# Two V loads and one V shift moved in the DMA order of a streaming-attention and feed-forward kernel

## The chip, the cores and the metric

One core of a Trainium2 chip runs the whole program. The metric is the device time of one execution in microseconds (us), as the median over executions. The engines are PE (TensorE), DVE (VectorE), ACT (ScalarE), POOL (GpSimd) and SP (SyncE). POOL and SP matter here because they issue DMAs: each takes its instructions strictly in order, so a DMA that waits for a semaphore holds up all that stands behind it.

## The reference

Attention over 4 batches, 8 heads, 768 positions and a head size of 64, then a feed-forward layer over the 3072 rows:

```python
scores = q @ k^T / 8                                # per batch and head
mask   = causal                       # heads 0, 2, 6 ("retrieval")
mask   = causal & (first 4 keys | last 64 keys)     # the other five ("streaming")
a      = softmax(where(mask, scores, -1e9))
x      = (a @ v), heads side by side                # [3072, 512]
h      = x @ w_in                                   # [3072, 2048]
out    = max(0.01 * h, h) @ w_out                   # [3072, 512]
```

## The kernel before

The rows are cut into eight chunks of 384 positions, two for each batch; chunk 4 is the first half of batch 2, chunk 5 its second half. A chunk passes through these stages: K, Q and V are loaded (converted to bf16), three pieces of 128 positions each; K and Q are turned, that is transposed, by DMA; K is spread by DVE into the score operand; the scores, their exponent and mask, and the product with V run on PE, ACT and DVE; the attention output is turned by DMA into `xt`; the two feed-forward products follow on PE.

The feed-forward products of earlier chunks are woven between the attention of the next one. That order is written out by hand: in pass n of the main loop the string `WOVEN[n]` (lines 602 to 609) names, letter by letter, the next piece of work from a list. In pass 3, `a` is an attention step of chunk 4, `t`, `A` and `B` are input products of chunk 3, `p` is an output product of chunk 2, `e` is the spreading of one third of chunk 5's K (line 274, DVE), and `v` is `v_shift(5)`.

V stands in two layouts. `va` is what `load_v` (line 118) loads on POOL's queue. `vb` is the same V moved by 64 positions, made by `v_shift` (line 146) with two DMAs, lines 150 and 151, for the streaming heads, whose window starts 64 positions early. `v_shift(4)` is issued on POOL, `v_shift(5)` on SP.

Two single buffers set the order of the loads: there is one `kb` and one `qb`, so the load of the next chunk's K waits until the present K has been turned, and the same for Q. `load_v` can take `behind=`: then POOL first copies one element of the tile named (line 121, into `hold`), and so waits until that tile has been written. Loads (`load_qk`, `load_v`) are on POOL's queue; turns (`turn_dma`, line 245), the turned attention outputs (line 443), the output stores (line 868) and most shifts are on SP's.

Around the change POOL's order is: load K and Q of chunk 4, load V of chunk 4 (line 1151), the sink values of batch 2 (line 133), `v_shift(4)`, load K and Q of chunk 5 (these in pass 2), then in pass 3 load V of chunk 5, load K of chunk 6, wait for the last output `xt` of chunk 4 (line 1187), load Q and V of chunk 6. SP's order in pass 3 is: turn K and Q of chunk 5, the four turned outputs of chunk 4 (heads 0 and 1, 2 and 3, 4 and 5, 6 and 7; here outputs 0 to 3), with stores between them, and `v_shift(5)` behind the fourth.

Behind output 3, pass 4 forms `x_sums` of chunk 4 on DVE (line 662), which read all four outputs; the product with `vb` of chunk 5 comes soon after (line 336).

Of the kernel before, what the change touches and what calls it, by code (L numbers as in the profile page):

```python
# [21 lines left out]
def kernel(  # L22
# [73 lines left out]
    raw = {}  # L96
# [13 lines left out]
    def load_qk(n, nms="kq"):  # L110
        b, c = ORDER[n]
        for nm in nms:
            t = rot.tile([128, 3, H, D], BF16, name=f"{nm}b", tag=f"{nm}b", bufs=1)
            raw[nm, n] = t
            for g in range(3):
                nc.gpsimd.dma_start(out=t[:, g], in_=nat[nm][b, c, :, :, g])  # L116

    def load_v(n, gs=range(3), behind=None):
        b, c = ORDER[n]
        if behind is not None:  # L120
            nc.gpsimd.tensor_copy(hold[0:1, :], behind)
        for g in gs:
            nc.gpsimd.dma_start(out=va[b][:, 3 * c + g, :, 0:D], in_=nat["v"][b, c, :, :, g])  # L123
# [3 lines left out]
    def load_sinks(b, eng=None):  # L127
        vsf[b] = vsfs[b % 2]
        (eng or nc.sync).dma_start(out=vsf[b].rearrange("(r f) d -> r f d", f=4)[:, 0], in_=v[b, :, 0:NS, :])

    def sink_values(b, eng):
        n = H - 1
        eng.tensor_tensor(
            vs[b % 2][:, 1:H, 0:D],
            vsf[b].rearrange("p (o d) -> p o d", o=1).to_broadcast([128, n, D]),
            m_sink[:, 1:H].rearrange("p (h o) -> p h o", o=1).to_broadcast([128, n, D]),
            op=ALU.mult)
# [8 lines left out]
    def v_shift(n, eng=None):  # L146
        eng = eng or nc.sync
        i, c = ORDER[n]
        lo, hi = (0, 2) if c == 0 else (2, 5)
        eng.dma_start(out=vb[i][0:64, lo:hi], in_=va[i][64:128, lo:hi, 1:H])  # L150
        eng.dma_start(out=vb[i][64:128, lo:hi], in_=va[i][0:64, lo + 1 : hi + 1, 1:H])
# [93 lines left out]
    def turn_dma(n, nms="kq"):  # L245
        for nm in nms:
            dst = rot.tile([128, 3, 4, 128], BF16, name=f"{nm}d", tag=f"{nm}d", bufs=3 if nm == "q" else 2)
            if nm == "q":
                qx[n] = dst
            else:  # L250
                raw["kx", n] = dst
            thirds = [slice(j, j + 1) for j in range(1 if nm == "q" and n == 3 else 3)]
            for g in thirds if n < 4 or (nm, n) == ("k", 4) else [slice(0, 3)]:
                nc.sync.dma_start_transpose(out=dst[:, g].rearrange("p g q t -> p (g q) t"),
                                            in_=raw[nm, n][:, g].rearrange("p g h d -> p (g h d)"))
# [8 lines left out]
    def spreads(n):  # L264
        b, c = ORDER[n]

        def spread(g, hh):
            r = slice(64 * hh, 64 * hh + 64)
            o = CH * c + 128 * g
            dst, src = kt[b % 2][hh][r, :, o : o + 128], raw["kx", n][r, g]  # L270
            if n == 2 and hh:
                nc.scalar.activation(out=dst, in_=src, func=ACTF.Copy)
            else:
                nc.vector.tensor_copy(dst, src)

        order = [(g, hh) for hh in range(2) for g in range(3)] if n < 4 else [(g, hh) for g in range(3) for hh in range(2)]
        r = [lambda g=g, hh=hh: spread(g, hh) for g, hh in order]
        if c == 0:
            r += sink_keys_by(b)
        return r  # L280
# [210 lines left out]
    class First:  # L491
# [109 lines left out]
    FIRST = "tttttttDttttL0tttt10Wt0kkk4k10k00k1k1S000k00S00aav011aSa22aa1Sa1a11a1aT1a11aa22a2a2eeaea2ee2eaa"  # L601
    WOVEN = {
        2: "aaptpIataatataatataqIataItaattIaaetaeapeaatatateaaepetteppe",
        3: "aappapapaxAppptAAaaAAtpAatAaaptaaBBAptpeeBaapaBBvetpBBpetetBe",
        4: "paappapapaxppaaApaatapatAaapAapAaAtpAaAeaeBpteeapapetaaABpeptpaBpBepatBptBpevBppppBpp",
        5: "paaxAteaAeatpaaAAtpIAaappaABApaatpBppeatBaeAIppaIeBBptpBItBtpBev",
        6: "axapAaApApaAAppApAaBapBBaAaBBpaaBpBapaCCaaCpaCBCapapCaaCDpapapDapppDpaDDpppDDDCppppp",
# [10 lines left out]
    def in_slots(n, tags=("ph",)):  # L618
        def tick(t, tag=None):
            ph = bank(tag or tags[t % len(tags)], [128, 512], FP32)  # L620
            for g in range(KG):
                nc.tensor.matmul(ph[:, 0:CH], lhsT=w_in_bf[:, g, 128 * t : 128 * t + 128],  # L622
                                 rhs=xts[n][:, g, :] if n else xts[0][:, :, g, :], start=(g == 0), stop=(g == KG - 1))
            done[n] += 1
            nc.scalar.activation(out=g_all[:, slab(n) : slab(n) + 3, t, :],  # L625
                                 in_=ph[:, 0:CH].rearrange("p (j t) -> p j t", j=3), func=ACTF.Prelu, alpha=0.01)

        ks = BY_SEVEN.get(n, ())
        ticks = [costing(0.65, lambda t=t: tick(t)) for t in range(NG) if t // 4 not in ks]
        if not n or n == 1:  # L630
            return ticks
        return {"t": ticks, **{"ABCD"[j]: Quad(n, k, ("psS" if j < 2 else "ph") if n + 1 == NCH else "ph", True).slots() for j, k in enumerate(ks)}}
# [24 lines left out]
    def x_sums(n):  # L657
        x = xts[n].rearrange("p g (j e t) -> p g j e t", j=3, e=2)
        b = lambda a, e: x[:, KH * a : KH * a + KH, :, e, :]
        t = rot.tile([128, 4, KH, 3, 64], BF16, name="x_sum", tag="x_sum", bufs=1)  # L660
        for i, y, z in ((1, b(0, 1), b(0, 0)), (2, b(1, 1), t[:, 0]), (3, b(1, 1), b(0, 1)), (4, b(1, 0), t[:, 1])):
            nc.vector.tensor_tensor(t[:, i - 1], y, z, op=ALU.subtract)
        x_sum[n] = t
        if n in (3, 4, 5):
            own = [rot.tile([128, CH], FP32, name=nm, tag=nm, bufs=1)[:] for nm in ("p1q", "uq")]
            t = rot.tile([128, 2, CH], FP32, name="s0", tag="kd", bufs=2)
            temps[n] = [own, [t[:, 0], t[:, 1]]]
        if n in (6, 7) and len(BY_SEVEN[n]) > 0:
            parts = [rot.tile([128, 2, CH], FP32, name=nm, tag=tag, bufs=bufs) for nm, tag, bufs in
                     (("s0", "kd", 2), ("s1", "kd", 2), ("s2", "kb", 1), ("s3", "qb", 1))]  # L670
            temps[n] = [[t[:, x] for x in range(2)] for t in parts]
# [255 lines left out]
    def steps(k, units=None):  # L927

        r = []
        for u in units or Pair.UNITS[pairs[k].duo]:  # L930
            for half in range(2):
                def step(u=u, half=half):
                    pairs[k].unit(u, half)
                    if not half:
                        return flush()
                    pending.extend((pairs[t], i) for t, i in sums_behind(k, u))
                    flush()
                r.append(costing(0.44, step))
        return r
# [208 lines left out]
        lists[c].pop(0)()  # L1148
    outs = lists.pop("2")
    assert not any(lists.values()) and not then_fourth  # L1150
    load_v(4)

    in_sums_left = [lambda i=i: in_sums(1, i + 1) for i in range(4)]
    for n in range(2, NCH):
        a, extra = [], []
        if n + 2 < NCH:
            if ORDER[n + 2][1] == 0:
                load_sinks(ORDER[n + 2][0])
                sink_values(ORDER[n + 2][0], nc.gpsimd)
            turn_dma(n + 2, {2: "k", 5: "q"}.get(n, "kq"))  # L1160
            if n == 3:
                load_v(n + 2, behind=raw["kx", n + 2][0:1, 0, 0, 0:1])
            if n == 4:
                v_shift(n + 2)
            extra = spreads(n + 2)
            if n == 2:
                v_shift(4, nc.gpsimd)
            if n + 3 < NCH:
                load_qk(n + 3, "k" if n > 2 else "kq")
        if n + 1 < NCH:  # L1170
            a = Attention(n + 1, cross=True).slots(lag=2 if n > 3 else 3)
        lists = {"a": a, "p": outs, "x": [lambda: x_sums(n)], "e": extra, "v": [], **in_slots(n)}
        if n in (3, 5):
            lists["v"] = [lambda: v_shift(n + 2)]
        if n == 2:
            lists["q"] = [lambda: turn_dma(4, "q")]
        if n == 4:
            lists["v"] = [lambda: turn_dma(7, "k")]
        if n in (5, 6):
            lists["I"] = in_sums_left  # L1180
        if n == 2:
            lists["I"] = [lambda i=i: in_sums(0, i + 1) for i in range(4)]
        for c in WOVEN[n]:
            lists[c].pop(0)()
        assert not any(lists[c] for c in lists if c not in "xI") and (n < 6 or not in_sums_left)
        if n in (3, 4):
            nc.gpsimd.tensor_copy(hold[0:1, :], xts[n + 1][0:1, 3, 0:1])
            load_qk(n + 3, "q")
            load_v(n + 3)
        outs = [f for k in range(3 * n // 2, 3 * n // 2 + 1 + n % 2) for f in steps(k)]  # L1190
# [36 lines left out]
```

## Time and profile before

| | us |
|---|---|
| median of 3 runs | 220.83 |
| lowest and highest | 219.82 to 221.55 |
| the profiled execution | 219.79 |
| its span, first to last instruction | 217.9 |

The span leaves 1.89 us outside it. In the profile a DMA has two times: that of its instruction on the issuing queue, and that from issue to landing, when its semaphore is complete. The number in brackets behind a row of the timeline is the engine's idle time just before it and what ended that. "SPq" and "POOLq" are the sequencers of SP and POOL.

### The profile page before, as it was taken

To read this page: it belongs to the slowest core of one execution; us is meant where nothing else is said; L and a number is where in the kernel's file an instruction comes from. 1 tells how busy PE (TensorE), PEld (TensorE's weight loads), DVE (VectorE), ACT (ScalarE), POOL (GpSimd) and SP (SyncE) were. 2 spreads that over 40 slices of the span, in tenths; PEclk is the share of its full clock that TensorE was granted. 3 is DMA by queue.
4 is the path that set the end of the run, shared out by engine and by line. 5 is a ranking of instruction groups with operands and counts; after the bars stand their busy time and mean duration, and the time that the engine had idled before them with its cause. 6 is when DMAs were issued, how large, how long until landed. Compare 5 with 4: busy or idle time off the path is not lost.

```text
span 217.9 us, 6313 instructions
## 1 busy us (share of the span) xinstructions
PE 210.0 (96%) x2524; PEld 174.8 (80%) x2524; DVE 165.9 (76%) x454; ACT 150.7 (69%) x348; POOL 74.1 (34%) x93
## 2 busy tenths in 40 slices
PE   8999999999999999899997999999999999999993
PEld 5678886678888676688785978788888999999893
DVE  6793787898699387788965875799996986977653
ACT  5768976764666996576686876686677995668420
POOL 8988463029707804806309700900000000000000
PEclk9999999999999999999999999999999999999999
DMA  9999999999999999999999999995140131200222
GB/s 131 153 175 170 185 207 192 172 163 116 169 145 237 180 117 156 174 162 155 103 186 175 138 139 188 169 172 99 50 137 3 21 110 43 101 0 3 96 102 90
DMA packets 112412, 28.79 MB, mean 132 GB/s; under 512 B 102208, under 2 KB 109376, under 8 KB 112384
## 3 DMA queue, kind: packets, MB, share of 16 engines
q0 software_dynamic: 78176, 13.61, 88.7%
q1 hardware_dynamic: 33152, 14.53, 36.0%
q8 instruction: 19, 0.31, 0.6%
q10 hardware_dynamic: 1056, 0.26, 0.6%
q14 instruction: 9, 0.07, 0.1%
HBM read 27.30 MB, written 6.29 MB: 154 GB/s over the span
## 4 chain that ended last, share of the span: by engine, by line
PE 66%; DMA 22%; POOL 6%; issue 2%; DVE 1%; SPq 1%; ACT 0%; POOLq 0%
PE py L834 15%; DMA va<-in_v_dram 11%; PE ph L622 10%; PE ph L710 8%; DMA kd<-kb 6%; PE po L336 4%; PE po L710 4%; PE py L813 4%; PE psS L368 3%; DMA kb<-in_k_dram 3%; DMA vb<-va 3%; PE ph L751 3%; PE psS L622 2%; PE po L813 2%; POOL kb L116 2%
## 5 line engine op out<-in xcount | busy, mean ns | idle before, releaser
L622 PE MATMUL ph<-xt,w_in_bf 128*128 128x384 bf16 x224 | 44.4, 326 | 0.0
L373 ACT ACTIVATE at<-psS 128x384 bf16<-128x384 f32 x73 | 34.0, 493 | 9.2 <-PE psS L368 8.6
L625 ACT ACTIVATE g_all<-ph 128x384 bf16<-128x384 f32 x56 | 27.5, 491 | 15.3 <-PE ph L622 14.5
L622 PEld LDWEIGHTS <-w_in_bf 128*128 128x128 bf16 x256 | 23.5, 98 | 11.2
L834 PEld LDWEIGHTS <-sum 128*128 128x128 bf16 x256 | 23.9, 98 | 2.5
L116 POOL DMA_DIRECT2D kb<-in_k_dram x21 | 18.9, 921 | 8.8 <-DMA kd<-kb 8.0
L123 POOL DMA_DIRECT2D va<-in_v_dram x24 | 21.4, 911 | 0.8 <-issue 0.7
L834 PEld LDWEIGHTS <-g_all 128*128 128x128 bf16 x192 | 17.9, 98 | 2.9 <-issue 0.2
L116 POOL DMA_DIRECT2D qb<-in_q_dram x21 | 18.6, 908 | 4.1 <-DMA w_in_bf<-in_moe_w_in_dram 1.9
L368 PE MATMUL psS<-qd,kt 128*128 128x384 bf16 (+2 forms) x81 | 19.1, 290 | 0.7 <-DMA qd<-qb 0.7
L336 PE MATMUL po<-va,at 128*128 128x65 bf16 x219 | 18.5, 194 | 0.0
L409 ACT ACTIVATE ats<-psS 128x384 bf16<-128x384 f32 x33 | 15.7, 490 | 2.6 <-PE psS L404 2.4
L336 PEld LDWEIGHTS <-at 128*128 128x128 bf16 x234 | 14.4, 98 | 3.7 <-issue 0.7
L834 PE MATMUL py<-w_sum,sum 128*128 128x256 bf16 x120 | 17.2, 272 | 0.0
L793 DVE TENSOR_TENSOR sum<-g_all 128x1024 bf16<-128x1024 bf16 x24 | 16.4, 685 | 0.7 <-ACT g_all L625 0.4
L834 PE MATMUL py<-w_out_bf,sum 128*128 128x256 bf16 x120 | 16.7, 272 | 0.0
L738 ACT ACTIVATE s<-ph 128x384 f32<-128x384 f32 x27 | 13.1, 492 | 5.1 <-PE ph L710 4.4
L834 PE MATMUL py<-w_out_bf,g_all 128*128 128x256 bf16 x112 | 16.1, 272 | 0.0
L438 DVE TENSOR_TENSOR xs<-po,linv 128x384 bf16<-128x384 f32 x27 | 15.1, 558 | 0.9
L413 DVE TENSOR_TENSOR ats<-ats,m_win 128x384 bf16<-128x384 bf16 x35 | 12.2, 356 | 4.3 <-ACT ats L409 3.7
L710 PEld LDWEIGHTS <-w_in_bf 128*128 128x128 bf16 x168 | 14.1, 98 | 0.9 <-issue 0.2
L710 PEld LDWEIGHTS <-in_sum 128*128 128x128 bf16 x160 | 13.5, 98 | 1.0
(250 smaller groups left out, 498.0 us busy)
## 6 DMA issues: line engine op xcount, KB each, us to landing
out_dram<-o SPq DMA_DIRECT2D x23, 256.0 KB, 2.3
va<-in_v_dram POOLq DMA_DIRECT2D x24, 128.0 KB, 7.0
qb<-in_q_dram POOLq DMA_DIRECT2D x21, 128.0 KB, 6.4
kb<-in_k_dram POOLq DMA_DIRECT2D x21, 128.0 KB, 6.6
w_out_bf<-in_moe_w_out_dram POOLq DMA_DIRECT2D x4, 512.0 KB, 13.0
w_in_bf<-in_moe_w_in_dram POOLq DMA_DIRECT2D x2, 512.0 KB, 8.9
w_in_bf<-in_moe_w_in_dram POOLq DMA_DIRECT2D x4, 256.0 KB, 8.1
vb<-va SPq DMA_DIRECT2D x6, 170.6 KB, 4.3
```

The costliest lines, as they stand in the source:

```text
L116: nc.gpsimd.dma_start(out=t[:, g], in_=nat[nm][b, c, :, :, g])
L123: nc.gpsimd.dma_start(out=va[b][:, 3 * c + g, :, 0:D], in_=nat["v"][b, c, :, :, g])
L336: nc.tensor.matmul(o, lhsT=lhsT, rhs=rhs, start=first, stop=False, skip_group_check=True)
L368: nc.tensor.matmul(s[:, off : off + w], lhsT=kt[i][hh][:, p, 128 * kj : 128 * kj + 128], rhs=q_of(n, p, lo, CH), start=(j == 0), stop=(j = ...
L373: nc.scalar.activation(out=a[:, 0:off], in_=s[:, 0:off], func=ACTF.Exp, scale=SM)
L409: nc.scalar.activation(out=av_, in_=s[:, 0:CH].rearrange("p (j e f) -> p j e f", j=3, e=2), func=ACTF.Exp, scale=SM)
L438: nc.vector.tensor_tensor(xs[:], po[:, :, :, 0:D], linv.to_broadcast([128, 3, 2, D]), op=ALU.mult)
L622: nc.tensor.matmul(ph[:, 0:CH], lhsT=w_in_bf[:, g, 128 * t : 128 * t + 128], rhs=xts[n][:, g, :] if n else xts[0][:, :, g, :], start=(g == ...
L625: nc.scalar.activation(out=g_all[:, slab(n) : slab(n) + 3, t, :], in_=ph[:, 0:CH].rearrange("p (j t) -> p j t", j=3), func=ACTF.Prelu, alp ...
L710: nc.tensor.matmul(s[:, 192 * m : 192 * m + 192], lhsT=lhs[:, g, 128 * m : 128 * m + 128], rhs=rhs[:, g], start=first and m == 0 and g == ...
L793: nc.vector.tensor_tensor(self.s[i], x, y, op=op)
L834: nc.tensor.matmul(s, lhsT=lhs[:, j, :], rhs=rhs[:, j, :], start=u in ("P1", "P2", "P5") and j == 0, stop=(j == NH - 1), skip_group_check= ...
```

## The change

The load of chunk 4's V gets a wait: POOL first copies one element of the third piece of chunk 4's Q (as loaded, not as turned). The load of chunk 5's V loses its wait for chunk 5's turned K, so it follows the load of chunk 5's Q directly in POOL's order. In pass 3's string the `v` moves from behind the fifteenth and last `a` to between the eleventh and the twelfth; by the slots of chunk 4, output 1 is sent at the tenth `a` and output 2 at the twelfth, so on SP the shift now stands between outputs 1 and 2.

```diff
-        3: "aappapapaxAppptAAaaAAtpAatAaaptaaBBAptpeeBaapaBBvetpBBpetetBe",
+        3: "aappapapaxAppptAAaaAAtpAatAaaptavaBBAptpeeBaapaBBetpBBpetetBe",
...
-    load_v(4)
+    load_v(4, behind=raw["q", 4][0:1, 2, 0, 0:1])
...
             if n == 3:
-                load_v(n + 2, behind=raw["kx", n + 2][0:1, 0, 0, 0:1])
+                load_v(n + 2)
```

## Rows read from the trace of the kernel before

**Rows 1.** Windows: stretch, length, PE, PEld, DVE, ACT, POOL busy, clock, DMA

```profile
110.00:120.00 10.00, 8.56 (x111) 6.83 (x109) 5.86 (x16) 7.41 (x18) 5.17 (x7) 1.00 1.41 185
...
sum 218.00, PE 209.99 PEld 174.75 DVE 165.93 ACT 150.66 POOL 74.14; mean PE 9.54 PEld 7.94 DVE 7.54 ACT 6.85 POOL 3.37
```

**Rows 2.** Timeline of PE: start, us, line, what, idle before

```profile
88.46 0.49 PE L368 MATMUL psS<-qd,kt 128*128 128x384 bf16 x3 [0.74 <-DMA qd<-qb]
...
94.56 0.19 PE L336 MATMUL po<-vb,ats 128*128 128x65 bf16 x1
...
108.92 0.49 PE L368 MATMUL psS<-qd,kt 128*128 128x384 bf16 x2
...
115.91 0.19 PE L336 MATMUL po<-vb,ats 128*128 128x65 bf16 x1 [1.44 <-DMA vb<-va]
```

**Rows 3.** Timeline of PE's weight loads at the second stall

```profile
115.87 0.25 PEld L336 LDWEIGHTS <-ats 128*128 128x128 bf16 x6 [1.75 <-DVE ats L413]
```

**Rows 4.** Timeline of DVE: K spread, output sums, mask

```profile
103.79 0.96 DVE L274 COPY kt<-kd 64x512 bf16<-64x512 bf16 x2
...
114.26 0.36 DVE L662 TENSOR_TENSOR x_sum<-xt,x_sum 128x384 bf16<-128x384 bf16 x1 [1.31 <-issue]
...
115.08 0.35 DVE L413 TENSOR_TENSOR ats<-ats,m_win 128x384 bf16<-128x384 bf16 x1
```

**Rows 5.** Chain of waits, 50 to 135 us: start, length, what

```profile
94.41 5.28 DMA kd<-kb
...
101.99 7.57 DMA va<-in_v_dram
...
109.58 6.19 DMA vb<-va
```

**Rows 6.** Timeline of POOL: the loads of chunks 4 and 5

```profile
69.22 2.65 POOL L116 DMA_DIRECT2D qb<-in_q_dram  x3
71.83 2.68 POOL L123 DMA_DIRECT2D va<-in_v_dram  x3
...
85.61 0.64 POOL L151 DMA_DIRECT2D vb<-va  x1 [0.35 <-DMA va<-in_v_dram]
86.24 2.79 POOL L116 DMA_DIRECT2D kb<-in_k_dram  x3
...
114.31 0.36 POOL L1187 COPY hold<-xt 1x1 bf16<-1x1 bf16 x1 [8.79 <-DMA xt<-xs]
```

**Rows 7.** Timeline of SP: two turns of Q, the last output

```profile
78.69 4.88 SPq L254 DMA_TRANSPOSE qd<-qb  x1
...
98.64 1.44 SPq L254 DMA_TRANSPOSE qd<-qb  x1
...
105.93 1.83 SPq L443 DMA_TRANSPOSE xt<-xs  x1
```

**Rows 8.** DMAs issued from 66 to 76: KB each, median us to landing

```profile
qb<-in_q_dram POOLq DMA_DIRECT2D x3, 128.0 KB, 7.6
va<-in_v_dram POOLq DMA_DIRECT2D x3, 128.0 KB, 11.2
...
kd<-kb SPq DMA_TRANSPOSE x3, 9.3
```

**Rows 9.** DMAs issued from 83 to 88: the outputs of chunk 3

```profile
xt<-xs SPq DMA_TRANSPOSE x3, 5.4
```

**Rows 10.** DMA queues from 72 to 77: packets, MB, share

```profile
q0 software_dynamic: 5475, 0.69, 219.3%
q1 hardware_dynamic: 103, 0.03, 3.5%
```

**Rows 11.** DMA queues from 77 to 83, same columns

```profile
q0 software_dynamic: 2484, 0.31, 142.2%
q1 hardware_dynamic: 1575, 0.38, 85.4%
```

**Rows 12.** DMA queues from 98 to 99, same columns

```profile
q1 hardware_dynamic: 869, 0.22, 99.4%
```

## The prediction

> **What bounds the kernel now.** I read the windows first. PE is busy for 209.99 us of the span, so a change off PE's path is worth only what PE now stands idle for, and one stretch stands out: of the ten us from 110 to 120 PE works 8.56 [rows 1]. PE's timeline then shows where. In the stretch that the change touches there are two stalls: 0.74 us before the first scores of chunk 4, which wait for its turned Q (the engine goes on at 88.46), and 1.44 us before the first product with chunk 5's shifted V (115.91) [rows 2]. Together 2.18 us: that is all that the change can win at PE in this execution.
>
> The chain of waits gives the origin of the second stall: K of chunk 5 lands, its turn takes 5.28 us from 94.41 (turned at 99.69), only then V of chunk 5 is issued, its last piece takes 7.57 us from 101.99 (109.56), and the shift 6.19 us from 109.58 (115.77) [rows 5]. The change aims at this chain.
>
> But a second chain ends almost at the same time, and the view of PE alone hides it. PE's weight load for that product waited for a mask of DVE's [rows 3]. DVE does that mask at 115.08, right behind the sums over chunk 4's outputs, and of these the second started at 114.26 after 1.31 us of idling [rows 4]. POOL's timeline says what came then: its wait for the last output of chunk 4 ended at 114.31 [rows 6], so that output landed at about 114.2. SP had issued it at 105.93 [rows 7]: 8.3 us to landing. So with V early and nothing else changed, the mask ends at 115.08 + 0.35 = 115.43 and PE goes on some 0.4 us sooner, not 1.44. The rest of the 1.44 is won only if output 3 lands sooner, and the change puts the shift ahead of that output on SP.
>
> **The change part by part.** *The wait of chunk 4's V.* Q of chunk 4 is issued in three pieces from 69.22 over 2.65 us; the last starts at about 71.0 and takes some 7.4 (median 7.6 [rows 8]), so it lands near 78.4. Today V is issued at 71.83 [rows 6]; then it is issued after the wait and the one-element copy (0.36 by the like copy in [rows 6]), at 78.9: 7 us later. It does not land 7 us later, since today its pieces queue behind Q and take 11.2 us [rows 8]. What V does meanwhile shows in the queues. From 72 to 77 the loads move 0.69 MB, 0.14 a us, and the turns next to nothing [rows 10]; from 77 to 83 loads and turns share the engines and move 0.31 and 0.38 MB, together 0.115 a us [rows 11]; a turn alone moves 0.22 in one us [rows 12]. Sharing costs: 0.31/0.14 + 0.38/0.22 is 3.9 us where the shared stretch took 6. With V held back, the turns run alone from about 77 until V's first bytes at some 81.3 (I take 2.4 us from issue to the first bytes). K's turn (three pieces of 0.13 MB) and most of Q's are through by then, and Q's turn, issued at 78.69 behind K's [rows 7], lands perhaps 2 us earlier than the 88.4 at which PE got it. That wins the 0.74 us; bounds 0 and -0.74, and I take -0.74.
>
> V of chunk 4 then lands, last piece: by the price of chunk 5's V today (7.57 us, issued beside a turn [rows 5]) 78.9 + 1.8 + 7.6 = 88.3; by the 11.2 of [rows 8] 91.9; by the bytes that are left (about 0.54 MB, at 0.115 to 0.17 a us from 81.3) 84.5 to 86. Today it lands at about 85.4, when the second half of its shift starts [rows 6]. I take 87, between the bytes and the first price: 1.6 us later, with -1 and +6.5 as bounds. Behind this wait POOL holds the sink values (1 us, wanted later), the shift of chunk 4 and the loads of K and Q of chunk 5: these move from 86.24 [rows 6] to 87.8. The shift, at 6.2 us, is there by about 93.5, and PE wants it at 94.56 [rows 2], or at 93.8 if the 0.74 was won: hidden, with little to spare. At the upper bound it costs 91.9 + 0.6 + 6.2 - 93.8, nearly 5 us.
>
> *Chunk 5's V straight behind its Q.* The copy into `hold` falls away (nothing on PE's path). V's issue starts at about 87.8 + 5.5 = 93.3 instead of 100.3. It now meets K's turn, which today runs nearly alone in 5.28 us [rows 5]. Chunk 4 today is the pattern for K, Q and V in a row: there the pieces of K's turn took 9.3 us and V's last piece landed some 18.9 us after K's issue began (66.5, 2.7 us ahead of Q's in [rows 6], to 85.4). For chunk 5 that gives V at 106.7; K turned at 95.9 + 9.3 = 105.2 where the trace shows 99.69, and by its own 5.28 at 101.2. DVE takes that K at 103.79 [rows 4]: a wait of 0 to 1.4 us on DVE; I take 0.5, and DVE's work ahead of output 3 moves by that. Chunk 5's turned Q is wanted at 108.92 [rows 2]; its turn moves from 98.64 [rows 7] to about 100.2 and with 5.3 to 9.3 us lands at 105.5 to 109.5: 0 to 0.6 us on PE, I take 0. K of chunk 6 waits for the turned K of chunk 5 as before and comes later, which nothing near it wants.
>
> *The shift between outputs 1 and 2.* Nothing else on SP moves, but SP stops at the shift until V has landed. The last V at 106.7 makes: second half of the shift issued until 107.4, output 2 until 108.7, output 3 issued at 108.7 where it is 105.93 [rows 7]; 2.8 us late. With V at 104 (the like of 7.6 us from its issue) it is 106, no loss. The shifted V itself lands near 107 + 6.2 = 113, before PE wants it at 114.47: the stall that the change is made of is gone. Output 3 takes 8.3 us today, beside the loads of V and of chunk 6's K; outputs with less beside them take 5.4 [rows 9]. Issued at 107.5, the middle of 106 and 108.7, it lands at 112.9 to 115.8; I take 114.8, nearer the upper price since K of chunk 6 still loads beside it: 0.6 us later than today.
>
> **The sum.** PE goes on 115.91 - 0.4 + 0.6 = 116.1 at the place of the second stall: +0.2 us, and the 0.74 won earlier is absorbed there, because that place is tied to a landing and not to PE's own pace. With the 0.5 of DVE's wait, which comes before output 3 is formed, +0.7. Behind it PE has no stall to lose or win against, so the end moves by +0.7: 219.79 + 0.7 = 220.5 for the profiled execution, which lies 1.04 below the median of the runs; against the median 220.83 + 0.7 = 221.5.
>
> **A rule weighed.** Loads and turns in [rows 11] slow each other down: 6 us for what takes 3.9 apart. The Trainium skill, "DMA: Bandwidth & Descriptors", section "Queues, rings and completion order", says that each DMA engine takes the queues that have work in turn, a packet from each. By that rule chunk 5's early V does not use idle engines but takes its share from K's turn, which would be the second rival below. [rows 10], where the turns' queue moved next to nothing beside the loads though two pieces of K's turn had been issued, agrees with it less well than [rows 11].
>
> **The rivals.** *Both stalls go (faster).* V of chunk 5 lands by 104, SP does not stop, output 3 keeps its 105.93 and, with V's load out of its way, takes 5.4 to 7 us: it lands by 113, and PE goes on at 113.7 to 114.5. -1.4 to -2.2 us: 218.6 to 219.4. For it: the 2 us that sharing costs in [rows 11] go to useful work. Against it: V must be there 5.5 us sooner than now although K and Q of chunk 5 start later.
>
> *V shares with K's turn and SP stops (slower).* Place: the shift on SP, with output 3 behind it, and the K spread on DVE. It decides from the point at which V lands after about 105. With V at 106.7 to 108, output 3 is issued at 108.7 to 110 and lands at 116.5 to 118 with the 8.3 us of today; DVE's sums, the mask and PE follow 1.3 us later, at 117.8 to 119.3. +2 to +3.4 us: 222.8 to 224.2. For it: chunk 4's own rows, 11.2 and 9.3 [rows 8]. Against it: K of chunk 6, which today loads beside output 3, then starts later and may leave the engines free.
>
> *Chunk 4's V is too late (slower).* It lands after 88.5, the shift after 94.7, and PE stalls at the first streaming product of chunk 4, by 1 to 4 us: 222 to 225. Against it: the turns that slowed V today are mostly done before it starts.
>
> *Nothing moves.* The second chain ends the stall as it does now: -0.4 to +0.3, 220.4 to 221.1. It is one end of the forecast.
>
> **Chances.** The forecast, with nothing moving (220.4 to 222.3): 0.48. Both stalls go: 0.21. SP stops: 0.24. Chunk 4's V late: 0.07. A measurement of this kernel tells about 1%, 2.2 us, from no change: under 218.6 or over 223.0. The first rival reaches 1% only where the timed executions stall longer than the profiled one (they take 1 us more at the median): 0.11 of its 0.21. Of the second and third about 0.25 of 0.31 lie above 223.0. So faster 0.11, same 0.64, slower 0.25. The range 218.6 to 224.0 leaves out about 0.1 on each side; the forecast's own is 220.4 to 222.3.
>
> **What would show it.** In the profile after: no stall of PE on chunk 4's turned Q near 88; V of chunk 4 issued near 79, landed near 87; K of chunk 5 issued near 88; V of chunk 5 landed near 105 to 107; output 3 issued at 106 to 109; and at PE's place of 115.91 a wait on DVE's mask instead of on the shifted V. Wrong is the forecast if V of chunk 4 lands by 85 (then all of chunk 5 comes earlier, and the first rival holds), or if the place of the longest wait is the K spread of chunk 5 or the first product of chunk 4.

## The result

The changed kernel is slower: 222.7 us at the median of 22 executions (220.34 to 227.0) against 220.34 for the kernel before (217.59 to 223.53), a ratio of 1.015 (95% interval 1.0121 to 1.018). The ratios here leave out executions well above the fastest ones of the same kernel (nine of the twelve with only the wait of chunk 4's V), and the medians hold all; where the two disagree both are given. In a second comparison it was 221.36 against 220.58, ratio 1.0044 (1.001 to 1.0079). Slower both times, and by an amount that differs from one set of executions to the next.

The profiled execution has a span of 221.7 us instead of 217.9. PE's timeline shows that both old stalls are gone and a new, longer one has come. The columns are those of [rows 2].

```profile
87.15 0.49 PE L368 MATMUL psS<-qd,kt 128*128 128x384 bf16 x3
...
104.62 0.49 PE L710 MATMUL ph<-x_sum,w_in_bf 128*128 128x192 bf16 x4
109.56 0.80 PE L710 MATMUL po<-xt,in_sum 128*128 128x192 bf16 x4 [4.44 <-DVE s L729]
...
114.29 0.49 PE L368 MATMUL psS<-qd,kt 128*128 128x384 bf16 x2
...
119.67 0.19 PE L336 MATMUL po<-vb,ats 128*128 128x65 bf16 x1
```

At 87.15 the first scores of chunk 4 no longer wait for their turned Q, and at 119.67 the first product with chunk 5's shifted V no longer waits: the 0.74 and the 1.44 of [rows 2] are gone from this execution. But ahead of the last input products of chunk 3 PE stands for 4.44 us. What it waits for is a sum of DVE's (line 729), so the next view is DVE's timeline:

```profile
102.15 0.41 DVE L839 TENSOR_TENSOR o<-py,u 128x256 f32<-128x256 f32 x1
107.30 0.59 DVE L274 COPY kt<-kd 64x512 bf16<-64x512 bf16 x2 [4.74 <-DMA kd<-kb]
...
108.96 0.55 DVE L729 TENSOR_TENSOR s<-po,s 128x384 f32<-128x384 f32 x1
```

DVE has nothing against that sum; it stands in order behind the spread of chunk 5's K (line 274), and that waits 4.74 us for K to be turned. Before, the same spread started at 103.79 without a wait [rows 4], since K had been turned at 99.69. Why K is late is read from POOL's timeline and the chain of waits:

```profile
79.92 0.18 POOL L121 COPY hold<-qb 1x1 bf16<-1x1 bf16 x1 [8.22 <-DMA qb<-in_q_dram]
80.37 2.64 POOL L123 DMA_DIRECT2D va<-in_v_dram  x3 [0.28 <-issue]
...
90.26 0.60 POOL L151 DMA_DIRECT2D vb<-va  x1 [0.68 <-DMA va<-in_v_dram]
90.86 2.67 POOL L116 DMA_DIRECT2D kb<-in_k_dram  x3
```

```profile
92.62 5.73 DMA kb<-in_k_dram
98.42 8.86 DMA kd<-kb
```

Two delays add up. The load of K is issued at 90.86 instead of 86.24 [rows 6], because on POOL it stands behind the shift of chunk 4's V, whose second half waits until that V has landed at about 90.2. And K's turn takes 8.86 us instead of 5.28 [rows 5]. It is issued at 98.42 and lands at 107.28, 7.6 us later than before: 4.0 from the start and 3.6 from the length. The queues of the DMA engines show what it shares with. In 98 to 101 the loads (here chunk 5's Q and V) move 0.41 MB and the turns' queue next to nothing:

```profile
q0 software_dynamic: 3280, 0.41, 222.0%
q1 hardware_dynamic: 13, 0.00, 0.7%
```

That is the picture of [rows 10], now on chunk 5, but it accounts for a part of the length only. In the kernel before the turn moved nothing at first either, for 1.7 us beside 0.26 MB of loads; here it was about 2.5 us. And the loads' queue was all but empty from about 102.5 on, yet the turn took 4.8 us more, where in the kernel before it took 3.2 us from 96.5, when the loads had passed. The turn of chunk 5's Q and two outputs were issued on the same queue in the meantime; what held the turn up there is not shown.

The stall has a price behind it as well. In windows of two us, PE's busy time and, third column from the end, the granted clock:

```profile
104.00:106.00 2.00, 1.12 (x11) 0.83 (x9) 0.00 (x0) 0.78 (x2) 0.00 (x0) 1.00 1.98 152
106.00:108.00 2.00, 0.00 (x0) 0.00 (x0) 0.66 (x3) 0.00 (x0) 0.17 (x1) 0.83 0.65 140
108.00:110.00 2.00, 0.44 (x4) 0.42 (x4) 1.66 (x5) 0.46 (x2) 2.00 (x3) 0.50 0.69 114
110.00:112.00 2.00, 2.00 (x11) 1.24 (x9) 1.56 (x5) 0.82 (x3) 0.46 (x1) 0.50 1.82 183
112.00:114.00 2.00, 2.00 (x9) 1.04 (x8) 0.40 (x2) 0.68 (x2) 0.00 (x0) 0.50 1.72 170
```

While PE stood still the clock fell to 0.50, the lower of its two levels (1.2 GHz of 2.4), and it stayed there until about 114. The same products, from the one at 109.56 to chunk 5's first scores at 114.29, took 4.73 us; before they ran from 106.42 to 108.92 [rows 2], 2.50 us:

```profile
106.42 0.49 PE L710 MATMUL po<-xt,in_sum 128*128 128x192 bf16 x4
```

So 2.2 us went to the clock. The account at PE: 1.3 us ahead before the stall, 4.4 lost in it, 2.2 lost to the clock, 1.4 won back at the shifted V: 3.9 us, where the spans differ by 3.8. Half of that lead of 1.3 is no part of the change: PE was already some 0.6 us ahead where chunk 4's Q came.

The fall does not follow in each execution. Of the 22, ten have a mean granted clock under 0.995, at a median of 224.2 us; the other twelve have a median of 221.8, still 1.5 us over the kernel before.

The same count over all timed executions, those of the experiments below included, supports the reading of one profile. In the four kernels where chunk 5's K stands on POOL behind a held-back V of chunk 4 (the changed kernel, the wait alone, the shift put back, the spreads at the end) 40 of 70 have a mean clock under 0.995. In the four kernels with chunk 5's V early but without that lateness it is 5 of 72, and in the kernel before, timed beside the experiments, 11 of 93. The shift alone, with 4 of 6, does not fit either group.

### The profile page after: what moved, and what is told of

Its sections match the earlier page's. It is cut to its first block, busy times and chain, and to the rows that moved or that the text cites. A ratio compares the mean times of both kernels' runs of the same rounds, so it can differ in the third digit from the quotient of the medians.

```text
span 221.7 us, 6314 instructions
## 1 busy us (share of the span) xinstructions
PE 210.9 (95%) x2524; PEld 175.5 (79%) x2524; DVE 166.3 (75%) x454; ACT 150.3 (68%) x348; POOL 73.6 (33%) x93
## 4 chain that ended last, share of the span: by engine, by line
PE 81%; DMA 11%; DVE 3%; POOL 2%; issue 1%; ACT 1%; SPq 0%; POOLq 0%
PE py L834 18%; PE ph L622 14%; PE ph L710 8%; PE py L813 7%; PE po L336 6%; PE psS L368 5%; DMA kd<-kb 4%; PE po L710 4%; DMA kb<-in_k_dram 3%; PE ph L751 2%; PE psS L622 2%; DMA va<-in_v_dram 2%; PE po L813 2%; PE psS L404 2%; DMA out_dram<-o 2%; PE po L834 2%
## 5 line engine op out<-in xcount | busy, mean ns | idle before, releaser
L622 PE MATMUL ph<-xt,w_in_bf 128*128 128x384 bf16 x224 | 45.6, 333 | 0.0
L622 PEld LDWEIGHTS <-w_in_bf 128*128 128x128 bf16 x256 | 23.9, 99 | 12.0 <-issue 1.0
L834 PEld LDWEIGHTS <-g_all 128*128 128x128 bf16 x192 | 18.4, 100 | 3.1 <-issue 0.3
L413 DVE TENSOR_TENSOR ats<-ats,m_win 128x384 bf16<-128x384 bf16 x35 | 12.8, 371 | 4.6 <-ACT ats L409 4.2
L722 ACT ACTIVATE g_all<-s 128x384 bf16<-128x384 f32 x23 | 11.9, 522 | 6.3 <-DVE s L729 6.2
```

Source lines behind the costliest of these rows:

```text
L834: nc.tensor.matmul(s, lhsT=lhs[:, j, :], rhs=rhs[:, j, :], start=u in ("P1", "P2", "P5") and j == 0, stop=(j == NH - 1), skip_group_check= ...
```

## The experiments

Each is timed beside the kernel before. The first group takes the three edits apart.

**The changed kernel without the wait of chunk 4's V.**

```diff
-    load_v(4, behind=raw["q", 4][0:1, 2, 0, 0:1])
+    load_v(4)
```

> The changed kernel without the wait of chunk 4's V: chunk 5's V straight behind its Q and the early shift stay. Theory (DVE waits for the turned K of chunk 5, which is late from two causes: its load starts 4.6 us late behind chunk 4's V, and its turn takes 8.9 instead of 5.3 us beside chunk 5's V): the load of K starts near 86.2 again, the turn from 94.4 still takes 8 to 9 us and ends near 103, DVE's wait shrinks from 4.7 to 0 to 1 us, PE's 4.4 us stall goes to under 1; total within 1.5 us of the kernel before, so about 2 to 4 us under the changed kernel. Rival 1 (SP stops at the early shift and output 3 of chunk 4 is late): still slower than before by 2 us or more, with PE's stall at the products that need the sums of chunk 4's outputs. Rival 2 (the turn beside V's load is alone enough): the wait on DVE stays over 3 us.

Measured: 219.41 against 220.48 at the median, ratio 1.0013 (0.9962 to 1.0065). Of POOL's timeline:

```profile
84.57 2.71 POOL L116 DMA_DIRECT2D kb<-in_k_dram  x3
...
102.00 2.66 POOL L116 DMA_DIRECT2D kb<-in_k_dram  x3 [9.49 <-DMA kd<-kb]
```

The load of chunk 5's K starts at 84.57. Its turn is as long as in the changed kernel (9.0 us), but it ends by 102.0, where the load of chunk 6's K, which waits for it, goes out; DVE's spread at 103.03 does not wait, and PE has no stall over 0.3 us from 80 to 120. So the wait of chunk 4's V is needed for the loss. The early shift on SP is not enough for it with V early: that rival, which wanted 2 us or more, falls. The rival that the long turn alone is enough falls too.

**Only the wait of chunk 4's V.** Chunk 5's V and the shift stay as in the kernel before.

> Only chunk 4's V waits for its Q; chunk 5's V is loaded behind its turned K and the shift stands behind output 3, as before. Theory: K of chunk 5 is loaded some 4 us later (near 90.5), its turn takes 5.3 us again and ends near 103.5, DVE waits 0.5 to 1.5 us for it; V of chunk 5 is issued near 104 and its shift lands near 119, where PE wants it at about 114: a stall of 4 to 5 us at the first product with the shifted V; total 2.5 to 5 us over the kernel before. Rival 1 (the early shift on SP is the cause): within 1 us of the kernel before.

Measured: 222.64 against 220.48 at the median, ratio 1.0029 (0.996 to 1.0097). K of chunk 5 is loaded at 91.15. Its turn, with no load of V beside it, takes 3.7 us and ends at 102.9; DVE does not wait for it. V of chunk 5, still behind that turn, is issued at 103.16, and PE pays at the shifted V:

```profile
117.98 0.19 PE L336 MATMUL po<-vb,ats 128*128 128x65 bf16 x1 [3.24 <-DMA vb<-va]
```

The direction and the place are as expected, the stall is 3.2 us where 4 to 5 were expected, the total 2.2 us over the kernel before where 2.5 to 5 were, and the 0.5 to 1.5 of DVE's wait were none. The clock fell to 0.50 behind this stall as well. So with the wait of chunk 4's V, and POOL's order as it is, the chain is late in both profiles: at K's spread with chunk 5's V early, at the shifted V without.

**Only chunk 5's V straight behind its Q.**

```diff
-                load_v(n + 2, behind=raw["kx", n + 2][0:1, 0, 0, 0:1])
+                load_v(n + 2)
```

> Only chunk 5's V is loaded straight behind its Q; chunk 4's V is not held back, the shift stands behind output 3. Theory: the turn of chunk 5's K starts near 94.4 as before and takes 8 to 9 us, ending near 103, so DVE waits under 1 us; V of chunk 5 lands near 103 to 105, the shift is issued at its old place near 108.5 and lands near 114, so the 1.4 us stall falls to 0.5 or less: total -1.5 to +0.5 us against the kernel before. Rival 2 (sharing with V alone makes K's turn too late): DVE waits over 3 us for it and the total is 2 us or more over the kernel before.

Measured: 219.23 against 220.48, ratio 0.9925 (0.9879 to 0.9971). K of chunk 5 is issued at 87.00 and turned in 7.9 us, by 103.1; DVE's spread at 104.39 does not wait, and PE does not stall at all from 90 to 120; what is left is 1.16 us at 89 for chunk 4's turned Q. This one edit of the three is a gain of just under 1%. One of its 12 executions took 309.02 us at a mean granted clock of 0.659; no trace shows why.

**Only the shift moved.** Chunk 4's and chunk 5's V are loaded as before.

> Only the shift of chunk 5's V moves between outputs 1 and 2 of chunk 4 on SP; both loads as before. SP then waits at the shift until chunk 5's V, issued near 100.3, lands near 109.5, and outputs 2 and 3 are issued near 111 to 113 instead of 103 and 105.9. Theory: output 3 lands near 117 to 119 instead of 114.2, the sums, the mask and PE's product with the shifted V follow, PE stalls 3 to 6 us there instead of 1.4, and the total is 2 to 5 us over the kernel before: the early shift needs the early V. Rival 5 (SP's order costs nothing): within 1 us of the kernel before.

Measured: 221.64 against 220.06, ratio 1.0102 (1.0041 to 1.0162), from 6 executions. SP stands at the shift until 110.03 and issues output 3 at 113.85, 8 us later than in [rows 7]; about 3.6 of these are older, since the spread of chunk 5's K starts, without a wait, at 107.41 instead of 103.79. DVE's sums wait 1.14 us for output 3 and PE 0.85 for the mask, where 3 to 6 were expected. Slower, by 1.6 us at the median where 2 to 5 were expected: output 3 had landed by 117.7, after 3.9 us instead of 8.3. The larger stall of this profile, 2.13 us at 86.7, lies ahead of the moved shift and belongs to the spread of chunk 4's K; it is not from this edit, and the clock fell to 0.50 behind it, so how much of the 1% belongs to the shift stays open.

**The changed kernel with the shift put back** behind output 3:

> The changed kernel with the shift of chunk 5's V put back behind output 3; chunk 4's V waits for its Q and chunk 5's V follows its Q. Theory (K of chunk 5 late and its turn beside V's load): the same stall as in the changed kernel, DVE waits 3 to 6 us for the turned K, total 221.5 to 224. Rival 1 (SP stops at the early shift): the stall goes and the total is within 1 us of the kernel before.

Measured: 221.38 against 220.06, ratio 1.0117 (1.0075 to 1.0159), just under the 221.5 to 224 expected.

```profile
108.85 0.67 PE L710 MATMUL po<-xt,in_sum 128*128 128x192 bf16 x4 [2.00 <-DVE s L729]
```

The same product waits for the same sum, 2.00 us, behind a spread that waited 2.30 for the turned K (under the 3 expected); the clock fell again. The two load edits together are enough for the loss, and it does not need the early shift. That the shift adds nothing in the changed kernel is not shown by this; its second profile, below, says otherwise.

The second group asks what of the late K costs.

**The spreads of chunk 5's K at the end of pass 3**, in the changed kernel:

```diff
-        3: "aappapapaxAppptAAaaAAtpAatAaaptavaBBAptpeeBaapaBBetpBBpetetBe",
+        3: "aappapapaxAppptAAaaAAtpAatAaaptavaBBAptpBaapaBBtpBBpttBeeeeee",
```

> The changed kernel with the six spreads of chunk 5's K moved from the middle to the end of pass 3's hand-written order, so that DVE takes the turned K after all the sums of that pass. Theory (PE's stall is DVE standing in order before the K spread): PE's 4.4 us stall ahead of the last input products of chunk 3 goes; DVE may wait under 1 us at the new place, and the first scores of chunk 5 by up to 2 us for the spreads; total 1.5 to 4 us under the changed kernel, -1 to +1.5 us against the kernel before. Rival 1 (SP stops at the early shift): no change from the changed kernel within 1 us. Rival 3 (the clock that fell is a cause of its own): granted clock still falls to 0.5 near 108 to 114 without a stall ahead of it.

Measured: 223.24 against 220.48 at the median, ratio 1.0048 (0.9992 to 1.0105): no better than the changed kernel by the medians. The old place is cured, as the theory said, but the time was not won:

```profile
118.83 0.20 PE L336 MATMUL po<-vb,ats 128*128 128x65 bf16 x1 [3.56 <-DVE ats L413]
```

```profile
109.39 0.64 SPq L150 DMA_DIRECT2D vb<-va  x1
110.56 0.60 SPq L151 DMA_DIRECT2D vb<-va  x1
111.28 1.59 SPq L443 DMA_TRANSPOSE xt<-xs  x1
112.97 0.92 SPq L868 DMA_DIRECT2D out_dram<-o  x1
114.00 1.21 SPq L443 DMA_TRANSPOSE xt<-xs  x1
```

Now PE stands 3.56 us at the next place: the mask behind the sums of chunk 4's outputs (DVE waits 3.86 us there), because SP issues output 3 at 114.00 instead of 105.93 [rows 7]. SP is late with everything from chunk 5's Q on: its turn went out at 102.17, then two outputs, the shift, output 2, a store, output 3. My expectation missed this. The late loads of chunk 5 reach PE by two ways, and taking away the first leaves the second, 3.6 us instead of 4.4. Here the early shift does stand in the way, from 109.39 to output 2 at 111.28, but as one of several in a line that began late. Behind this stall the granted clock stays at 1.00, though nine of the 12 executions have a mean under 0.995.

**Chunk 5's K loaded ahead of the shift of chunk 4's V**, in the changed kernel:

```diff
             if n == 2:
+                load_qk(n + 3, "k")
                 v_shift(4, nc.gpsimd)
             if n + 3 < NCH:
-                load_qk(n + 3, "k" if n > 2 else "kq")
+                load_qk(n + 3, "k" if n > 2 else "q")
```

> The changed kernel with one thing moved: on POOL the load of chunk 5's K stands ahead of the shift of chunk 4's V instead of behind it, so it no longer waits until chunk 4's V has landed. Theory (the wait of chunk 4's V costs by what is queued behind it on POOL: K and Q of chunk 5): K of chunk 5 is issued when K of chunk 4 is turned, near 83 to 85 instead of 90.9, its turn ends near 98 to 102 instead of 107.3 and DVE's 4.7 us wait for it goes; Q of chunk 5 still stands behind the shift, near 91, so its turn ends near 104 to 107, just ahead of the first scores of chunk 5; total 1 to 4 us under the changed kernel, -1.5 to +1.5 us against the kernel before. Rival 1 (SP stops at the early shift of chunk 5's V): no change from the changed kernel within 1 us. Rival 2 (the turn beside loads alone): the turn still takes over 8 us, DVE waits over 2 us.

Measured: 220.22 against 220.06, ratio 1.0003 (0.996 to 1.0046). All three edits of the change are in this kernel, and the loss is gone:

```profile
82.58 2.68 POOL L123 DMA_DIRECT2D va<-in_v_dram  x3 [0.28 <-issue]
86.13 2.70 POOL L116 DMA_DIRECT2D kb<-in_k_dram  x3
...
92.25 0.61 POOL L151 DMA_DIRECT2D vb<-va  x1 [0.40 <-DMA va<-in_v_dram]
```

V of chunk 4 lands at about 92.2 (this execution is 2.4 us behind the changed kernel's already at the load of chunk 4's K), but K goes out at 86.13, is turned in 7.5 us by 103.5, and DVE's spread at 106.77 does not wait. What is left of the wait is a stall of 1.08 us at 97.53, on the shifted V of chunk 4, which the prediction had named as the place where a late V would show; 0.62 us at 95.24 went to a late output of chunk 3. So the wait of chunk 4's V cost by what stood behind it on POOL, more than by the lateness of that V.

**The same move without the wait of chunk 4's V**, with only chunk 5's V early:

> Chunk 5's V straight behind its Q, no wait for chunk 4's V, the shift of chunk 5's V at its old place (the best form so far), and chunk 5's K loaded ahead of the shift of chunk 4's V. Theory: K is issued 1 to 3 us sooner than 86 to 87, its turn ends 1 to 3 us sooner, but the shift of chunk 4's V moves behind its issue by under 1 us; PE has no stall left there but the one for the turned Q of chunk 4, so nothing is won: within 1 us of 219.3. Rival 4 (chunk 4's K and Q turns lose to chunk 5's K, loaded beside them): the stall ahead of chunk 4's first scores grows from 0.7 to 1.2 us to over 2 and the total is 1 us or more slower than that.

Measured: 220.37 against 220.06, ratio 1.0035 (0.999 to 1.0079). K went out at 87.15 and had waited 6.49 us for chunk 4's K to be turned, so nothing was won at its start, and its turn took 11.3 us. The stall ahead of chunk 4's first scores did not grow as the rival said, but PE lost 1.5 us at 86.6 behind a mask that follows the spread of chunk 4's K. So the move wins where the load stands behind a late V, and here it does not.

**The best form, and the changed kernel, once more on one chip:**

> The kernel with only chunk 5's V loaded straight behind its Q, measured a second time beside the changed kernel, to see whether it beats both. Theory: no stall over 0.5 us between 100 and 120, median 0.5 to 1.8 us under the kernel before and 2 to 4 us under the changed kernel, and hardly any run with a mean granted clock under 0.995. Rival (its lead was chance): within 0.4 us of the kernel before.

> The changed kernel without the wait of chunk 4's V, a second time, beside the form without the early shift. Theory: with chunk 5's V landed before SP comes to the shift, its place on SP is worth nothing: within 0.5 us of the form with the late shift. Rival: the early shift delays outputs 2 and 3 and costs 1 us or more.

> The changed kernel as it is, beside the two forms above on the same chip. Theory: median 2 to 3 us over the kernel before; DVE waits 3 to 5 us for the turned K of chunk 5, and about half of its runs show a mean granted clock under 0.995. Rival (the stall was that of one execution): no wait over 1 us on DVE for that K in this profile.

Measured, against 220.58 for the kernel before: only chunk 5's V early 218.41, ratio 0.9914 (0.9875 to 0.9953); with the early shift too 220.19, ratio 0.9947 (0.9902 to 0.9992); the changed kernel 221.36, ratio 1.0044 (1.001 to 1.0079). The first beats the kernel before by 1.3 and 2.2 us at the median in its two comparisons (0.5 to 1.8 were expected of the second), with one of 12 executions under a mean clock of 0.995, and the changed kernel by 3.0 where both were run. What the early shift costs there stays open: its medians are 0.2 and 1.8 us above the form without it, where under 0.5 was expected. Its second profile has PE wait 0.47 us at 116.08 for the mask behind output 3, issued at 111.14; the form without it, with output 3 issued at 107.05, has no stall there. The changed kernel is 0.8 us over the kernel before at the median, where 2 to 3 were expected. Its second profile has a DVE wait of 1.22 us for the turned K, outside the 3 to 5 that the theory expected, and nearly the rival's bound of 1:

```profile
104.70 0.59 DVE L274 COPY kt<-kd 64x512 bf16<-64x512 bf16 x2 [1.22 <-DMA kd<-kb]
...
114.92 0.36 DVE L662 TENSOR_TENSOR x_sum<-xt,x_sum 128x384 bf16<-128x384 bf16 x1 [1.43 <-DMA xt<-xs]
```

Its turn took 7.3 us instead of 8.9, and it started 1.0 us sooner. What this costs PE is split between two places:

```profile
106.96 0.49 PE L710 MATMUL po<-xt,in_sum 128*128 128x192 bf16 x4 [0.92 <-DVE s L729]
...
116.14 0.20 PE L336 MATMUL po<-vb,ats 128*128 128x65 bf16 x1 [1.14 <-DVE ats L413]
```

The first is the stall of the first profile, 0.92 us instead of 4.44. The second, and longer, is the mask behind output 3, which SP issued at 111.23 and which landed at about 114.8: SP's order costs something in the changed kernel too. This execution is the second shortest of its 12, with the span of the kernel before, 217.9, so it shows how the loss can be absent more than how it arises. Six of the 12 have a mean granted clock under 0.995.

Over all profiles the length of chunk 5's K turn falls into two groups, by one edit. With chunk 5's V held back until the turn is done: 5.3 (before), 3.7 (only the wait of chunk 4's V), 5.8 (only the shift). With V straight behind Q: 7.3 to 11.3 in ten profiles.

## Why the prediction came out as it did

The measured median lies inside the stated range, and the time moved the way that the point forecast did. But the forecast's own range was 220.4 to 222.3, and its verdict, no change that can be told, was given the most chance; the first comparison says 1.5%. Its own sign of being wrong came true as well: in the first profile the longest wait is at the spread of chunk 5's K. That the number fell inside the wide range is partly luck, since in the profiled execution a wait that was priced too low and a clock that was not priced at all made up the time. Step by step:

- *The two old stalls, 2.18 us at most to win.* Both are gone from the first profile after. That the wait of chunk 4's V wins the first is not shown: of the seven profiles without that wait, five have no stall on chunk 4's turned Q either.
- *The second chain behind the second stall* (output 3, its sums, the mask). Right as a mechanism: it ends PE's stall with the spreads late (3.56 us), with only the shift moved (0.85), and in the changed kernel's second profile (1.14), at the place that the prediction named. In the first profile after it is not what decides, since the stall at the K spread comes earlier.
- *V of chunk 4 lands at 87.* Mis-sized, by 3 us. Q landed at 79.8 instead of 78.4, and V took 7 to 8 us from each issue, so its last piece landed near 90.2. The price by the nearest row, 7.57 us, gave 88.3, and I chose a value under it because of the bytes left over. Of the 3 us, 1.5 are the later issue (80.37 instead of 78.9), and most of the rest is the landing taken below that row.
- *K of chunk 5 issued at 87.8.* Follows from that: 90.86. That the wait moves the loads behind it on POOL was the right step; the size was 4.6 us instead of 1.6.
- *K's turn, 5.28 to 9.3 us.* The bounds held (8.86), but from the later start they gave 103.7 to 107.7, not 101.2 to 105.2.
- *DVE's wait, 0.5 of 0 to 1.4.* This is the term that failed: 4.74. The 0.5 stood for a K turned at 104.3. It was turned at 107.28, 3.0 us later: 2.5 from the start of the turn (98.42 instead of 95.9) and 0.5 from its length (8.86, where the 0.5 stands for about 8.4). The other 1.2 us came from DVE itself, which was ready for that K at 102.56 instead of 103.79, since PE ran ahead. So it was the late start, out of the first edit, more than the sharing, that broke the term.
- *What DVE's wait does to PE.* I let it delay only output 3. The trace shows that PE itself stands behind the K spread, through the sum of line 729 queued after it. The price was therefore not what is left of the wait at the end of a chain, but nearly all of it, at once: 4.44 of 4.74 us.
- *The clock.* Not in the sum at all: 2.2 us in this execution.
- *The second rival* named the K spread on DVE and the shift on SP as the places, and 222.8 to 224.2 as the time. The first place is right. At the second, SP did not stop for V, as the rival had it: in both profiles the shift went out straight behind output 1 (108.02 and 106.77), and only with the shift alone did SP wait there. Output 3 was late all the same, from the line on SP, and decides in the second profile alone. The rival's number was about right for partly another reason, so it doesn't count as shown; its sum also holds a slip, since 108.7 and 110 with 8.3 us give 117 to 118.3 and so 223.2 to 224.5.

On the rule weighed in the prediction (the Trainium skill, "DMA: Bandwidth & Descriptors", "Queues, rings and completion order": the engines take the queues with work in turn, a packet from each): the runs agree that loads and turns share, with 3.7 to 5.8 us for the turn without V's load beside it and 7.3 to 11.3 with it. In one stretch the share is even by packets, from 98.5 to 99.5 in the kernel without the wait of chunk 4's V:

```profile
q1 hardware_dynamic: 418, 0.11, 80.4%
q0 software_dynamic: 412, 0.05, 79.5%
```

In another it is not: from 98 to 101 in the changed kernel the turn, already issued, moved next to nothing beside 0.41 MB of loads. The runs don't show whether it had packets ready in its first us.

## What to carry to other kernels

Ask of a wait that is added to a queue not only when the transfer behind it lands, but what else stands in that queue and who waits for that: here chunk 5's K, behind that V's shift, was worth more than the V that was held back. A transfer that is moved to share with another has to be costed together with whatever moves that other's start, since two delays of a few us each use up a slack of 4 us that either alone would leave. And where an instruction on a shared engine may wait, count each instruction queued behind it as waiting as well, before asking what the end of the chain costs.

## What I had not expected of the hardware

A stall of PE could cost more than its length: after 4.44 us of idling the granted clock was at 0.50 until about 114, and the next products took 4.73 us instead of 2.50. It also fell to 0.50 behind a stall of 2.00 us (the shift put back) and one of 2.13 (the shift alone), each time once PE was working again, and stayed at 1.00 behind one of 3.56 (the spreads at the end). In the changed kernel 16 of its 34 timed executions show the lower mean clock. So the length of the stall alone does not tell whether the clock falls. A DMA turn beside the loads of Q and V took 7.3 to 11.3 us in ten profiles, and 3.7 to 5.8 in the three where V was held back until it was done.
